# Spreading the DMA transposes of a batch over four head pairs, and placing the sums of the next quad behind different products

## Chip, cores and metric

The kernel runs on one core of one Trainium2 chip. The metric is device time in microseconds (us) of that core; smaller is better. A ratio is the mean time of one kernel's fast runs over the mean of the other's fast runs of the same rounds, so it is not quite the ratio of the medians quoted beside it.

## The reference

Grouped attention, then a feed-forward with a squared ReLU:

```python
# q: 8 x 16 heads x 384 x 64, k and v: 8 x 4 heads x 384 x 64
k = np.repeat(k, 4, axis=1); v = np.repeat(v, 4, axis=1)
scores = np.matmul(q, k.transpose(0, 1, 3, 2)) / 8
scores = scores - scores.max(-1, keepdims=True)
attn = np.exp(scores); attn = attn / (attn.sum(-1, keepdims=True) + 1e-9)
x = np.matmul(attn, v)                    # to 3072 tokens x 1024
h = np.maximum(x @ w_in, 0.0)             # w_in  1024 x 2048
out = (h * h) @ w_out                     # w_out 2048 x 1024
```

## The kernel before

A recorder takes every operation in program order, works out semaphore waits from named keys, and writes one in-order program for each engine. A batch is eight head pairs (`c` = 0 to 7). The feed-forward runs in the same TensorE stream, on two halves of 64 rows side by side: one batch behind attention at first, later two.

Three parts matter here.

First, a batch ahead, q and k are turned by DMA transposes. They are all issued by SyncE, the engine that also issues the transposes `xT` of each pair's attention result and all stores of the output:

```python
def prepare(b):                       # of batch b, one batch ahead
    dup_all_k(b, "gpsimd")            # copies k_st twice into k_dup
    ...dma_start_transpose(kT[b % 2] <- k_dup)                  # all of k
    for part in range(2):
        ...dma_start_transpose(qT[b % 2] half <- q_st[1] half)  # four pairs each

# main loop over head pairs, n = 8 * b + c
    if NPB < n < (B - 1) * NPB:
        if c == (4 if b > 1 else 6):
            prepare(b + 1)
# loads of k, q, v of batch b + 1: once the xT transpose of pair c = 0 has landed
#   row_attend(n - 1, load_next if c == 1 and 2 <= b < B - 1 else None)
```

Second, the down projection of batches 2 to 7 works on quads of blocks with seven products (a Strassen-like scheme) and four sums on VectorE. Where one quad follows another, which happens three times (in the feed-forward of batches 3, 5 and 7), the sums of the following quad are made during the products of the present one:

```python
def rest(q, early, follow):           # products 6, 7, (2), 5, 4 of quad q
    def sums_ahead():
        if follow: sum_part(follow, (1, 2, 3))       # three in a row
    until(sums 1, 2, 3, 4 of q are made)
    ...product 6: y add
    def p7(acc, key):
        add(q["v"], q["u"], acc, key)
        if early: sums_ahead()
    ...
    def c22(acc, key):                # behind product 5
        add(y, q["v"], acc, key); store(y, ...)
        if follow: sum_part(follow, (4,))
    def c21(acc, key): ...            # behind product 4: subtract, store
# then product 1 of the following quad, then product 3 of q (p3: add, store)
```

Third, the output tiles `y_sb` are a fixed ring of six; a store is recorded as soon as its tile is ready:

```python
def next_y():
    ys[0] += 1
    return ys[0] % NY                 # NY = 6
```

The softmax here doesn't subtract the row's maximum and nothing guards it: scores larger than these inputs give would overflow.

## Time and profile before

| | before |
|---|---|
| time, first three runs | 417.27 us median (416.78 to 417.67) |
| span of the profiled run | 415.2 us, granted clock 1.000 |
| TensorE busy | 407.2 us |
| issue time that all matmuls need (worked out below) | 393.2 us |

The page of the kernel before has this for its span, TensorE's share and the chain of work that ended last:

```profile
span 415.2 us, 13254 instructions
...
PE 407.2 (98%) x6061; PEld 307.3 (74%) x6061; DVE 206.6 (50%) x458; ACT 214.1 (52%) x281; POOL 48.7 (12%) x62
...
PE 91%; DVE 4%; ACT 2%; DMA 1%; issue 1%; ACTq 0%; POOL 0%; DVEq 0%
```

TensorE bounds the kernel, but "98% busy" hides slack, because matmuls overlap: the records of one last 376 ns while another starts every 216 ns on the same half. A better measure is the step from one start to the next when nothing holds the stream: 216 ns for 512 columns, 162.5 for 384, 32 for 65. Summed, with two halves side by side, that is 393.2 us. I call it a **stand** when neither half has a matmul in its step, worked out from the start times. I call **head** the time from the span's start to the first scores of batch 1 (35.85 us here), and **rest** what follows (379.37 us).

The first stand that the change aims at. This is the chain of waits of the kernel before near 214 us (start us, us, what):

```profile
210.96 0.69 DVE y_sb L622
211.65 0.61 DVE a_late L622
...
212.90 0.69 DVE h2T L622
...
213.72 0.57 DVE o_sb L527
...
214.33 0.20 PE po L517
```

VectorE adds a product to its output tile, then makes three sums in a row (two into `a_late`, one into `h2T`), and only then gets to `o_sb`, which empties the one PSUM bank `po` that the next attention product needs. TensorE stands 0.69 us. The same happens near 313 us (0.48) and near 398 us (0.46), together 1.63 us.

The second, near 231 us. ScalarE's own timeline in the kernel before (the last bracket is its idle time and what ended it):

```profile
225.40 1.13 ACT L504 ACTIVATE expT<-sc_ps 128x1152 bf16<-128x1152 f32 x1 [1.53 <-PE sc_ps L500]
229.17 0.58 ACT L740 COPY y_sb<-f_ps 128x512 f32<-128x512 f32 x1 [2.64 <-PE po L517]
229.65 1.14 ACT L504 ACTIVATE expT<-sc_ps 128x1152 bf16<-128x1152 f32 x1
```

The releaser in the bracket is misleading: ScalarE's record just before the copy, at 229.11, is a wait for the semaphore of an output store. That store had left SyncE at 221.40 and landed at 229.09, 7.7 us later against a median of 2.3. The copy waits because the ring gives it the tile that was stored last. The Exp behind it is late by as much, and TensorE stands 1.44 us. From 217.6 to 230.3 the load of q for the next batch was under way.

The list of DMA issues has the sizes of the whole run (count, median us from issue to landing):

```profile
qT<-q_next SPq DMA_TRANSPOSE x12, 5.0
...
kT<-k_dup SPq DMA_TRANSPOSE x6, 7.0
```

### The profile page before, as it was taken

To read this page: it belongs to the slowest core of one execution; us is meant where nothing else is said; L and a number is where in the kernel's file an instruction comes from. 1 tells how busy PE (TensorE), PEld (TensorE's weight loads), DVE (VectorE), ACT (ScalarE), POOL (GpSimd) and SP (SyncE) were. 2 spreads that over 40 slices of the span, in tenths; PEclk is the share of its full clock that TensorE was granted. 3 is DMA by queue.
4 is the path that set the end of the run, shared out by engine and by line. 5 is a ranking of instruction groups with operands and counts; after the bars stand their busy time and mean duration, and the time that the engine had idled before them with its cause. 6 is when DMAs were issued, how large, how long until landed. Compare 5 with 4: busy or idle time off the path is not lost.

```text
span 415.2 us, 13254 instructions
## 1 busy us (share of the span) xinstructions
PE 407.2 (98%) x6061; PEld 307.3 (74%) x6061; DVE 206.6 (50%) x458; ACT 214.1 (52%) x281; POOL 48.7 (12%) x62
## 2 busy tenths in 40 slices
PE   8999999999999999999999899999999999999997
PEld 4666888788787787787766688787876788679643
DVE  2664433378332567255563446545654445535453
ACT  4855864377654566546544556555654544214200
POOL 5831002022003000300012000300000000000000
PEclk9999999999999999999999999999999999999999
DMA  8999999859429920991029930496012210020022
GB/s 233 197 197 202 205 190 183 187 80 151 86 87 130 187 70 21 106 226 50 11 82 160 166 108 11 54 199 139 11 48 96 96 47 11 2 101 2 27 77 102
DMA packets 96104, 45.03 MB, mean 108 GB/s; under 512 B 74416, under 2 KB 90032, under 8 KB 96048
## 3 DMA queue, kind: packets, MB, share of 16 engines
q0 software_dynamic: 34288, 16.65, 32.0%
q1 hardware_dynamic: 58720, 25.28, 29.3%
q10 hardware_dynamic: 3040, 2.26, 1.8%
q8 instruction: 47, 0.77, 0.7%
q14 instruction: 9, 0.07, 0.1%
HBM read 35.65 MB, written 12.58 MB: 116 GB/s over the span
## 4 chain that ended last, share of the span: by engine, by line
PE 91%; DVE 4%; ACT 2%; DMA 1%; issue 1%; ACTq 0%; POOL 0%; DVEq 0%
PE sc_ps L558 18%; PE f_ps L558 17%; PE sc_ps L688 12%; PE po L517 12%; PE f_ps L688 11%; PE sc_ps L500 7%; PE sc_ps L604 5%; PE f_ps L604 4%; PE f_ps L843 2%; DMA w_late<-in_q_dram 1%; ACT expT L504 1%; PE po L378 1%; DVE y_sb L622 1%; PE sc_ps L361 1%; PE sc_ps L300 1%
## 5 line engine op out<-in xcount | busy, mean ns | idle before, releaser
L504 ACT ACTIVATE expT<-sc_ps 128x1152 bf16<-128x1152 f32 x112 | 126.5, 1130 | 106.7 <-PE sc_ps L500 64.1
L558 PE MATMUL f_ps<-xT,w_in_sb 64*128 64x384 bf16 x976 | 150.2, 322 | 0.0
L558 PE MATMUL sc_ps<-xT,w_in_sb 64*128 64x384 bf16 x976 | 149.2, 322 | 0.0
L558 PEld LDWEIGHTS sc_ps<-xT,w_in_sb 64*128 64x128 f16 x976 | 81.8, 94 | 16.0
L558 PEld LDWEIGHTS f_ps<-xT,w_in_sb 64*128 64x128 f16 x976 | 82.6, 94 | 13.3
L517 PEld LDWEIGHTS po<-v_aug,expT 64*128 64x128 bf16 x2016 | 77.4, 94 | 12.2 <-DVE o_sb L527 2.2
L568 ACT ACTIVATE h2T<-hr 128x384 bf16<-128x384 f32 x122 | 61.3, 519 | 47.0 <-DVE hr L564 46.5
L517 PE MATMUL po<-v_aug,expT 64*128 64x65 bf16 x2016 | 81.4, 190 | 0.8 <-DVE o_sb L527 0.8
L500 PE MATMUL sc_ps<-qT,kT 64*128 64x384 bf16 x336 | 56.9, 323 | 2.0 <-ACT expT L504 1.8
L564 DVE TENSOR_SCALAR hr<-sc_ps 128x384 f32<-128x384 f32 x61 | 33.9, 556 | 37.1 <-PE sc_ps L558 16.3
L564 DVE TENSOR_SCALAR hr<-f_ps 128x384 f32<-128x384 f32 x61 | 33.9, 556 | 30.1 <-PE f_ps L558 14.5
L688 PE MATMUL sc_ps<-w_late,h2T 64*128 64x512 f16 x176 | 43.5, 376 | 0.0
L604 PE MATMUL sc_ps<-w_out_sb,h2T 64*128 64x512 f16 x192 | 41.6, 376 | 0.0
L604 PE MATMUL f_ps<-w_out_sb,h2T 64*128 64x512 f16 x192 | 40.6, 376 | 0.0
L688 PE MATMUL f_ps<-w_out_sb,a_late 64*128 64x512 f16 x160 | 39.5, 376 | 0.0
L688 PE MATMUL f_ps<-w_out_sb,h2T 64*128 64x512 f16 x144 | 35.4, 376 | 0.0
L688 PE MATMUL sc_ps<-w_out_sb,h2T 64*128 64x512 f16 x144 | 35.4, 376 | 0.0
L525 DVE RECIPROCAL rinv<-po 128x6 f32<-128x6 f32 x56 | 11.0, 196 | 47.0 <-PE sc_ps L604 12.8
L527 DVE TENSOR_TENSOR o_sb<-po,rinv 128x384 bf16<-128x384 f32 x56 | 31.2, 557 | 1.9
L500 PEld LDWEIGHTS sc_ps<-qT,kT 64*128 64x128 bf16 x336 | 25.0, 94 | 8.9 <-ACT expT L504 4.8
L688 PE MATMUL f_ps<-w_late,h2T 64*128 64x512 f16 x112 | 27.2, 376 | 0.0
L688 PE MATMUL sc_ps<-w_out_sb,a_late 64*128 64x512 f16 x112 | 26.9, 376 | 0.3 <-DVE y_sb L622 0.3
(101 smaller groups left out, 418.0 us busy)
## 6 DMA issues: line engine op xcount, KB each, us to landing
out_dram<-y_sb SPq DMA_DIRECT2D x47, 256.0 KB, 2.3
q_next<-in_q_dram POOLq DMA_DIRECT2D x7, 768.0 KB, 10.6
w_in_sb<-in_moe_w_in_dram POOLq DMA_DIRECT2D x8, 512.0 KB, 12.4
w_out_sb<-in_moe_w_out_dram POOLq DMA_DIRECT2D x2, 2048.0 KB, 33.6
k_st<-in_k_dram POOLq DMA_DIRECT2D x7, 192.0 KB, 4.0
v_st<-in_v_dram POOLq DMA_DIRECT2D x7, 192.0 KB, 11.2
xT<-o_sb SPq DMA_TRANSPOSE x56, 2.7
w_late<-in_q_dram ACTq DMA_DIRECT2D x1, 768.0 KB, 8.4
```

Source lines behind the costliest of these rows:

```text
L300: m = pe.matmul(ps[:, t * 128:(t + 1) * 128], src[:, t * 128:(t + 1) * 128], ident[:], is_transpose=True)
L500: "tensor", lambda pe: pe.matmul(sc_ps[:, i, 0:S], kt[rows, j * 128:(j + 1) * 128], qt[rows, :]),
L504: R.add("scalar", lambda e: e.activation(expT[p % NEX][:, 3 * half:3 * half + 3, :], sc_ps[:, 0:3, 0:S], AF.Exp, scale=0.125), reads=[("sc ...
L517: "tensor", lambda pe: pe.matmul(po_v[:, f % NJ, f // NJ, :], expT[p % NEX][rows, 2 * j + f % 2, f // 2 * 128:f // 2 * 128 + 128], v_aug[b ...
L525: R.add("vector", lambda e: e.reciprocal(rinv_v, po_v[:, :, :, D:D + 1]), reads=["po"], writes=[("rinv", p % 2)])
L527: R.add("vector", lambda e: e.tensor_tensor(o_sb[p % NO][:, :, :, :], po_v[:, :, :, 0:D], rinv_v.to_broadcast([128, NJ, 2, D]), ALU.mult), ...
L558: "tensor", lambda pe: pe.matmul(acc[:, 0:S], w_in_sb[rows, kc, c * 128:(c + 1) * 128], xT[b % NXT][rows, kc, :], start=(h == 0 and kc == ...
L564: R.add("vector", lambda e: e.tensor_scalar_max(hr[r][:, :], acc[:, 0:S], 0.0), reads=[key], writes=[("hr", r)])
L568: R.add("scalar", lambda e: e.activation(h2T[b % 2][:, c, :], hr[r][:, :], AF.Square), reads=[("hr", r)], writes=h2(b, c))
L604: "tensor", lambda pe: pe.matmul(acc, h2T[b % 2][rows, c, i * 128:(i + 1) * 128], w_out_sb[rows, c, jj * 512:(jj + 1) * 512], start=(h == ...
L688: "tensor", lambda pe: pe.matmul(acc, lhs[rows], right[rows, c], start=(first and h == 0 and c == 0), stop=(h == 1 and c == NHC - 1), skip ...
L843: m = pe.matmul(acc[:, 0:S], w_in_sb[:, kc, c * 128:(c + 1) * 128], xT[b % NXT][:, kc, :], start=(kc == 0), stop=(kc == NKC - 1))
```

## The change

The intent: shorter bursts on SyncE and on the DMA engines, and no long run of sums on VectorE. The transposes of a batch become six (k in two, q in four), spread over pairs 4 to 7. For batch 2 all six still go out at once, at pair 6, where before three did. The sums 1, 2, 3 and 4 of the following quad go behind products 7, 5, 4 and 3, one each. Product 6 accordingly asks for sums 1 to 3 alone.

```diff
-    def prepare(b):
-        dup_all_k(b, "gpsimd")
-        ...one transpose of k, two of q
+    def turn_k(b, g): ...      # transpose of two k heads
+    def turn_q(b, c): ...      # transpose of two head pairs of q
+    PARTS = [(turn_k, 0), (turn_q, 0), (turn_q, 2), (turn_k, 2), (turn_q, 4), (turn_q, 6)]
+    def prepare(b, parts=range(6)):
+        for i in parts: ...
@@ def p3: behind product 3
             store(q["u"], x0, i0, 1)
+            if follow:
+                sum_part(follow, (4,))
@@ def rest
-                sum_part(follow, (1, 2, 3))
+                sum_part(follow, which)          # ahead(which)
@@ behind product 7 (or 2)
-                sums_ahead()
+                ahead(1)
@@ behind product 5
-            if follow:
-                sum_part(follow, (4,))
+            ahead(2)
@@ behind product 4
+            ahead(3)
@@ main loop
             if c == (4 if b > 1 else 6):
-                prepare(b + 1)
+                dup_all_k(b + 1, "gpsimd")
+            if b == 1 and c == 6:
+                prepare(2)
+            if b > 1 and c >= 4:
+                prepare(b + 1, ((0,), (1, 2), (3, 4), (5,))[c - 4])
```

## The prediction

> **What bounds the kernel now.** TensorE: the page gives PE 98% busy over 415.2 us and 91% of the chain that ended last, at clock 1.00. As busy time of pipelined matmuls hides slack, I counted issue steps from the trace: two 64-row streams run side by side, a matmul every 216 ns (512 columns), 162.5 ns (384) or 32 ns (65). All matmuls together need 393 us. The other 22 us are lost: about 12.5 in the first 40 us, 4 in the last 10, only 5.5 between. The change touches that middle and the start of the tail.
>
> **Gaps it can reach** (both streams idle; start times and the chain of waits):
> 1. Near 214, 313 and 398 us TensorE stands 0.71, 0.52 and 0.54 us, together 1.77. The chain is VectorE: y add 0.69, three sums of the next quad 0.61 + 0.61 + 0.68 in a row, then reciprocal 0.20 and o_sb 0.56 (at 398 the next y add), then the matmul that needs the bank.
> 2. Near 231 us it stands 1.45 us behind an Exp queued behind the ScalarE copy of product 2, which waits for an output store to leave its y buffer: issued 221.4, landed 229.1, 7.7 us against the usual 2.3. From 219 to 226 us the queue of the q load holds the DMA engines.
> 3. About 1.5 us of small gaps (exp latency at 78, 130, 134; others); not addressed.
>
> **What the change does.** Sums: same number and size; one each behind products 7, 5, 4, 3 instead of three behind 7 and one behind 5. VectorE has about 2.7 us between an attend's end and the next one's need of the bank; y add + one sum + reciprocal + o_sb take 2.1, so most of (1) goes: -1.5 us. No product comes close to waiting for its sum.
> Transposes: 3 issues per batch (k about 2.9 us of SyncE, q twice 2.2) become 6, in five of six prepared batches over four head pairs: +18 issues of an estimated 1.2 to 2 us, on SyncE, off the chain. They no longer block SyncE while q lands (a ready store waited 6 us at 230), so xT transposes and stores land earlier, but none of these is on the chain. The late store of (2) was issued before the k transpose and starved by the q load, which stays. The Trainium skill, "DMA: Bandwidth & Descriptors", section "Queues, rings and completion order", says that each DMA engine round-robins between queues per packet and a completion lands only after that engine's earlier writes; the 7.7 us agree with sharing, hardly with fair turns. Indirectly (2) shrinks by about 0.5: with the sums apart, the transpose that triggers the q load comes about 1.2 us earlier, the chain 0.7. PE's 3 more waits per batch hide behind queued matmuls.
>
> **Sum.** -1.5 - 0.5 = -2.0 us: 417.3 to **415.2 us**, 80% range 413.7 to 416.9. Faster by over 2%: 0.01; within 2%: 0.98; slower by over 2%: 0.01.
>
> **What would show it.** The gaps near 213, 312, 397 us gone, VectorE showing y add + one sum; the same matmuls in the same order; a store near 228 us still landing after about 7 us and the ScalarE copy waiting for it, 0.7 to 1.2 us of stall; k transposes 12 (was 6), q 24 (was 12), in all slightly more SyncE issue time; head and end unchanged.
>
> **What would make it wrong.** The store stall vanishing (then about 414) or growing, because the y buffer's need and the q load move against each other; a sum behind product 4 or 3 delaying an o_sb into a new stall of half a us; late k and q parts landing after the next batch's scores need them.

## More of the kernel before

What SyncE does near 70 us, where batch 2 is prepared (its queue in the timeline; x is the number of issues merged in a line):

```profile
64.55 2.59 SPq L331 DMA_TRANSPOSE kT<-k_dup  x1
68.56 3.94 SPq L338 DMA_TRANSPOSE qT<-q_next  x2
72.54 1.56 SPq L396 DMA_TRANSPOSE xT<-o_sb  x1
74.14 2.08 SPq L589 DMA_DIRECT2D out_dram<-y_sb  x3
76.26 2.50 SPq L396 DMA_TRANSPOSE xT<-o_sb  x2
```

The q transposes wait for the q load, which lands at 68.5; then come the `xT` transposes of the last three pairs of batch 1, with three stores between.

## The result, and the profile after

The changed kernel took 416.59 us median (415.77 to 418.48, six runs) against 417.35 (416.71 to 417.67, six runs) of before; ratio 0.9992, 95% interval 0.9969 to 1.0014. That is not the 415.2 predicted. Two later sets of the same kernel, each against the kernel before on the same chip, gave 1.0039 (1.0010 to 1.0068) and 1.0017 (0.9996 to 1.0038). The mean of the three sets is 417.77 us, that of before in the same sets 417.19: if anything, the change costs half a us.

The page of the changed kernel, same three lines:

```profile
span 414.9 us, 13294 instructions
...
PE 406.6 (98%) x6061; PEld 310.9 (75%) x6061; DVE 208.0 (50%) x458; ACT 214.2 (52%) x281; POOL 48.1 (12%) x62
...
PE 91%; DMA 4%; DVE 2%; ACT 2%; ACTq 0%; issue 0%; POOL 0%; DVEq 0%
```

The chain lost half of its VectorE share and got four times the DMA share. The matmuls and their order are the same in the two programs. In this profile the rest of the span fell from 379.37 to 377.71 us, and the head grew from 35.85 to 37.16.

VectorE's timeline of the changed kernel in the place of the first stand:

```profile
213.30 0.69 DVE L630 TENSOR_TENSOR y_sb<-sc_ps,y_sb 128x512 f32<-128x512 f32 x1 [1.55 <-PE po L525]
213.91 0.68 DVE L630 TENSOR_TENSOR a_late<-h2T 128x1024 bf16<-128x1024 bf16 x1
214.51 0.19 DVE L533 RECIPROCAL rinv<-po 128x6 f32<-128x6 f32 x1
214.73 0.56 DVE L535 TENSOR_TENSOR o_sb<-po,rinv 128x384 bf16<-128x384 f32 x1
```

One sum instead of three now stands ahead of `o_sb`. The stands near 214 and 398 us are gone; 0.22 us is left near 313.

The output store near 223 us, in the chain of waits of the changed kernel:

```profile
223.04 6.65 DMA out_dram<-y_sb
...
229.76 0.59 ACT y_sb L748
230.35 1.04 ACT expT L512
...
231.43 0.49 PE sc_ps L508 x3
```

It is still late (6.65 us), and in this profile the stand was 0.39 us. SyncE's queue where batch 2 is prepared:

```profile
65.11 1.22 SPq L331 DMA_TRANSPOSE kT<-k_dup  x1
68.38 3.35 SPq L339 DMA_TRANSPOSE qT<-q_next  x2
71.78 1.29 SPq L331 DMA_TRANSPOSE kT<-k_dup  x1
73.11 3.81 SPq L339 DMA_TRANSPOSE qT<-q_next  x2
76.97 1.26 SPq L404 DMA_TRANSPOSE xT<-o_sb  x1
78.27 1.56 SPq L597 DMA_DIRECT2D out_dram<-y_sb  x3
79.87 2.51 SPq L404 DMA_TRANSPOSE xT<-o_sb  x2
```

From the landing of q (68.4) on, the transposes hold the queue until 76.9 instead of 72.5: q takes four issues instead of two, and the second half of k, which before went out with the first while q was still loading, now waits between them. The last `xT` is issued at 81.1 instead of 77.5. And this is on the chain, in a place where before there was no stand. Chain of waits of the changed kernel:

```profile
80.72 0.40 DVE y_sb L620
81.12 2.37 DMA xT<-o_sb
83.49 0.04 issue
83.53 0.33 PE sc_ps L566
```

Line 566 is the up projection of batch 1; it needs the last `xT` of that batch, and TensorE stands 1.01 us. The list of DMA issues:

```profile
qT<-q_next SPq DMA_TRANSPOSE x24, 3.7
...
kT<-k_dup SPq DMA_TRANSPOSE x12, 4.3
```

Each part lands sooner, as intended; it does not help, because the whole of a batch is not wanted sooner.

### The profile page after: what moved, and what is told of

The parts are those of the page before. It is cut to its first block, busy times and chain, and to the rows that moved or that the text cites. A ratio compares the mean times of both kernels' runs of the same rounds, so it can differ in the third digit from the quotient of the medians.

```text
span 414.9 us, 13294 instructions
## 1 busy us (share of the span) xinstructions
PE 406.6 (98%) x6061; PEld 310.9 (75%) x6061; DVE 208.0 (50%) x458; ACT 214.2 (52%) x281; POOL 48.1 (12%) x62
## 4 chain that ended last, share of the span: by engine, by line
PE 91%; DMA 4%; DVE 2%; ACT 2%; ACTq 0%; issue 0%; POOL 0%; DVEq 0%
PE sc_ps L566 18%; PE f_ps L566 17%; PE f_ps L696 12%; PE sc_ps L696 12%; PE po L525 12%; PE sc_ps L508 7%; PE sc_ps L612 5%; PE f_ps L612 4%; DMA w_late<-in_q_dram 2%; DMA out_dram<-y_sb 2%; PE f_ps L854 2%; PE po L386 1%; ACT expT L512 1%; PE sc_ps L369 1%; PE sc_ps L300 1%; DMA xT<-o_sb 1%
## 5 line engine op out<-in xcount | busy, mean ns | idle before, releaser
L525 PEld LDWEIGHTS po<-v_aug,expT 64*128 64x128 bf16 x2016 | 77.4, 94 | 10.8 <-DVE o_sb L535 0.9
L533 DVE RECIPROCAL rinv<-po 128x6 f32<-128x6 f32 x56 | 10.9, 195 | 46.1 <-PE sc_ps L612 12.8
## 6 DMA issues: line engine op xcount, KB each, us to landing
q_next<-in_q_dram POOLq DMA_DIRECT2D x7, 768.0 KB, 10.8
w_in_sb<-in_moe_w_in_dram POOLq DMA_DIRECT2D x8, 512.0 KB, 11.9
```

What stands on the lines that cost most here:

```text
L525: "tensor", lambda pe: pe.matmul(po_v[:, f % NJ, f // NJ, :], expT[p % NEX][rows, 2 * j + f % 2, f // 2 * 128:f // 2 * 128 + 128], v_aug[b ...
L533: R.add("vector", lambda e: e.reciprocal(rinv_v, po_v[:, :, :, D:D + 1]), reads=["po"], writes=[("rinv", p % 2)])
```

## The experiments

My theory after the result (A): the moved sums are worth 1.4 to 1.5 us; the six transposes of batch 2 at once cost about 1 us; the late store and the head vary by chance. Rivals: all of the new loss is chance (B), or the sums or the smaller transposes themselves cost time (C).

The table has one profile of each run, in us. For e1 to e4 these are the first profiles, with spans of 417.0, 414.2, 415.5 and 414.7 us; the traces that are kept for these four are of other executions (416.0, 413.3, 415.8 and 415.2 us). The kept ones are a second sample, given below the table. "Sums" adds the stands near 214, 313 and 398; "84", "97" and "231" are the other stands that differ; "mean" is over all runs of that set, "before" that of the kernel before in the same set.

| kernel | head | rest | sums | 84 | 97 | 231 | mean | before |
|---|---|---|---|---|---|---|---|---|
| before | 35.85 | 379.37 | 1.63 | 0 | 0 | 1.44 | 417.24 | |
| e5 before again | 35.94 | 378.93 | 1.63 | 0 | 0 | 1.00 | 417.12 | 416.97 |
| e9 before, one instruction more | 36.30 | 379.99 | 1.63 | 0 | 0.66 | 1.31 | 417.00 | 417.48 |
| e14 before, v load later | 36.49 | 378.74 | 1.64 | 0 | 0 | 0.80 | 417.69 | 417.39 |
| e6 before, tiles in order of stores | 36.34 | 377.82 | 1.63 | 0 | 0 | 0 | 416.01 | 416.97 |
| e3 six parts only | 35.91 | 379.63 | 1.63 | 0.91 | 0 | 0.82 | 418.14 | 416.95 |
| e2 sums only | 36.27 | 377.90 | 0.22 | 0 | 0 | 1.57 | 417.17 | 416.95 |
| the change | 37.16 | 377.71 | 0.22 | 1.01 | 0 | 0.39 | 416.89 | 417.23 |
| e1 the change again | 38.16 | 378.81 | 0.22 | 0 | 0 | 2.52 | 418.57 | 416.95 |
| e13 the change, third set | 36.66 | 378.36 | 0.23 | 0.54 | 0 | 1.48 | 417.86 | 417.39 |
| e4 change, batch 2 mended | 36.67 | 377.99 | 0.22 | 0 | 0 | 1.70 | 416.66 | 416.95 |
| e11 e4, loads a pair earlier | 36.13 | 376.20 | 0.23 | 0 | 0 | 0 | 415.28 | 417.48 |
| e10 change, tiles in order | 36.58 | 377.14 | 0.23 | 0.73 | 0 | 0 | 415.76 | 417.48 |
| e8 e4, tiles in order | 36.48 | 376.18 | 0.23 | 0 | 0 | 0 | 414.81 | 416.97 |
| e7 sums only, tiles in order | 38.02 | 376.24 | 0.23 | 0 | 0 | 0 | 414.75 | 416.97 |
| e12 e7 again | 36.07 | 376.99 | 0.23 | 0 | 0.66 | 0 | 414.59 | 417.48 |
| e15 e7, more warm-up | 36.77 | 377.00 | 0.22 | 0 | 0.66 | 0 | 415.46 | 417.39 |

The table checks itself: take the 376.2 us of e8 as a base, add 1.4 where the sums are not moved, and add the stands 84, 97 and 231; every rest comes out within 0.45 us. The kept traces of e1 to e4, read in the same way, do so too:

| kept trace | head | rest | sums | 84 | 97 | 231 |
|---|---|---|---|---|---|---|
| e1 the change again | 36.64 | 379.36 | 0.22 | 1.87 | 0 | 1.11 |
| e2 sums only | 35.97 | 377.30 | 0.22 | 0 | 0 | 0.94 |
| e3 six parts only | 36.58 | 379.22 | 1.63 | 0.78 | 0 | 0.52 |
| e4 change, batch 2 mended | 36.79 | 378.39 | 0.23 | 0 | 0.66 | 1.34 |

### e1, the changed kernel again

No edit.

> The changed kernel once more, to separate chance from cause. In the first profile of it the head (span start to the first scores of batch 1) took 37.2 us against 35.9 before, and the rest 377.7 against 379.4. Theory A (the head is chance of the first DMAs, the 1.0 us stand of TensorE near 84 us is caused by the change): the head comes out anywhere from 35.5 to 37.5 us, the rest again at 377.7 within 0.3, the stand near 84 us is there again with 0.7 to 1.3 us, those near 214 and 398 us are gone. Rival B (the stand near 84 us is chance too): it is absent or of another size, and the rest is near 376.7. Rival C (the change itself slows the head): the head is 37 us again. Time 416.0 to 417.3 us.

Measured: ratio 1.0039, rest 378.81, head 38.16, none near 84 us, 2.52 near 231 us. Both the stand near 84 and the rest missed theory A's numbers. The stand near 84 is not fixed: the q load that opens SyncE's burst landed at 68.8 us, as in the first profile (68.4), since it sits behind the weight loads on the DMA queue and not behind TensorE (in the kept traces it landed at 68.0 to 69.8 us whatever the head; at 68.6 in e7 with a head of 38.02). With a head 1.0 us later TensorE comes 1.0 us later to an `xT` that lands even earlier (82.9 against 83.5). Counted from the end of the head, the last `xT` landed 46.33 us on in the first profile (stand 1.01), 46.22 in e3 (0.91), 46.04 in e10 (0.73), 45.86 in e13 (0.54) and 44.73 in e1 (none): in each case the stand is the landing less 45.3 us, where TensorE needs it. In the kept traces of kernels without the six at once it landed at 42.5 to 44.3, always in time. So a late head hides this stand, and a late q load makes it longer: in the kept trace of e1 q landed at 69.7 us, the last `xT` 47.25 us after the head, and TensorE stood 1.87 us in two pieces (0.85 and 1.02, for the last two `xT`). In that of e3 it was 46.09 and 0.78.

### e2, sums only

The transposes as before; the rest of the diff stays.

> Only the move of the sums; transposes as before (three at once). Theory A: the sums are worth about 1.5 us and, through the earlier q load, part of the store stall; no stand near 84 us. Rest of the span 376.7 to 377.2 us (before 379.4), stands near 214 and 398 gone, 231 between 0.3 and 1.2. Time about 2 us under before when the head is equal. Rival C (what the first result gave back came from the sums, not the transposes): a stand near 84 us also here, rest 377.7. A smaller stand near 231 than 0.9 would mean that the sums, not the spread transposes, took that stall away.

Measured: rest 377.90, no stand near 84, sums' stands 0.22 instead of 1.63, near 231 us 1.57. Time 416.68 median, ratio 1.0006 (0.9984 to 1.0027). The sums do what was predicted, to a tenth; the store stand did not shrink in this profile (0.94 in the kept trace; the kernel before had 1.44 and 1.00). The rival that the sums make the stand near 84 falls. The time of this set is not faster than before. Two of its six runs (419.23 and 418.09 us) had a lowered clock; what else took the gain back in the runs without a trace is not shown, the head and the store being the likely places (see e7, and the clock below).

### e3, six parts only

The sums as before; the transposes as in the change.

> Only the six parts of the transposes; sums as before. Theory A: the stand near 84 us is there (0.7 to 1.3 us), those near 214, 313 and 398 us as before (together about 1.65), 231 near the 1.44 of before, since the late store was issued ahead of any transpose; rest 380.2 to 380.6 us, so about 1 us slower than before with an equal head. Rival (the spread transposes took the store stall away): 231 shrinks to about 0.4, and the rest is near 379.4.

Measured: stand near 84 us 0.91, near 231 us 0.82, rest 379.63; time 417.97 median, ratio 1.0033 (1.0020 to 1.0046). The parts alone make the kernel slower, by 1.2 us in the mean (418.14 - 416.95), and bring the stand near 84 with them. The rest came out better than expected because the store stand was smaller, as it can be in the kernel before too (e14: 0.80; 0.52 in the kept trace of e3, with a rest of 379.22).

### e4, batch 2's last parts behind the last xT

```diff
             if b == 1 and c == 6:
-                prepare(2)
+                prepare(2, (0, 1, 2))
+            if b == 2 and c == 0:
+                prepare(2, (3, 4, 5))
```

> The changed kernel with the last three of batch 2's six parts issued behind the last two xT transposes of batch 1 (same transposes, same bytes, another place in SyncE's order). Theory A (SyncE works in order, so the last xT, which the feed-forward of batch 1 waits for, is issued 3.6 us later than before): the last xT is issued near 77.5 us instead of 81.1, the stand near 84 us is gone, rest 376.6 to 376.9 us, about 1 us less than the changed kernel. Rival (six smaller transposes load the DMA engines more, whatever their order): the stand stays at 0.5 us or more.

Measured: the stand near 84 us is gone. SyncE's queue in this kernel:

```profile
71.50 1.26 SPq L404 DMA_TRANSPOSE xT<-o_sb  x1
72.80 3.19 SPq L597 DMA_DIRECT2D out_dram<-y_sb  x3
76.03 2.52 SPq L404 DMA_TRANSPOSE xT<-o_sb  x2
78.59 1.29 SPq L331 DMA_TRANSPOSE kT<-k_dup  x1
```

The same six transposes of the same bytes, in another place in the order, and the last `xT` is issued at 77.3. So it was the order on SyncE and not the load on the DMA engines. The kept trace agrees: last `xT` issued at 77.8, no stand near 84. The rest was 377.99 and not 376.6 to 376.9, all of it because the store stand was 1.70 here.

### e5, control: the kernel before again

No edit.

> Control: the kernel before, unchanged, in the place of a variant. So far the variants' runs scatter over 1.7 to 4.9 us each, those of before over 1.1. Theory A (the scatter comes from the landing of the first inputs and of the late store, which are chance, in every kernel): ratio 1.000 within 0.003, the head (35.9 us in the one profile of before) anywhere from 35.5 to 38, the stand near 231 us anywhere from 0.4 to 2.5 us. Rival (the change itself makes head and stand unsteady): head 35.9 and stand 1.4 again within 0.2, all runs within 416.5 to 417.7 us.

Measured: ratio 1.0006 (0.9992 to 1.0019), all runs 416.67 to 417.58, head 35.94, store stand 1.00. Neither theory is met whole: the store stand moves by 0.4 between two profiles of one kernel, but head and times of the kernel before are steady. The scatter of the changed kernels is larger and asks for a reason.

### e6, the kernel before with tiles in the order of their stores

```diff
-    ys = [0]
+    ys = list(range(NY))
     def next_y():
-        ys[0] += 1
-        return ys[0] % NY
+        return ys.pop(0)
@@ def store
+        if c1 == 512:
+            ys.append(y)
```

Every tile is stored once, so the tile handed out is the one whose store was issued longest ago.

> The kernel before, with the y buffers handed out in the order in which their stores were issued instead of in a fixed ring, so that the ScalarE copy of product 2 takes a buffer whose store is long done. Theory A (that copy waits for the store behind the q load, and nothing else holds the Exp near 231 us): the stand near 231 us is gone, the others (214: 0.69, 313: 0.48, 398: 0.46) stay; rest 377.9 to 378.1 us, 1.4 us under before. Rival (the Exp would be late anyway, behind DMAs): the stand stays over 0.7 us.

Measured: no stand near 231 us, the others unchanged, rest 377.82; ratio 0.9980 (0.9966 to 0.9994). The copy now starts at 227.40, its store dependence gone, while the store after product 3 still landed 7.0 us after its issue. So the wait for the tile was all that held the Exp.

### e7 and e12, moved sums and tiles in order, transposes as before

The edits of e2 and e6 together.

> The moved sums, transposes as before, y buffers in the order of their stores. Theory A (sums -1.5 us, store stall -1.4 us, independent): rest 376.2 to 376.5 us against 379.4 of before, and less scatter than the sums alone. If the gain of the sums is given back in the late store, as the sums-only runs suggest (416.7 against 416.9), this one shows the full 3 us: ratio 0.992 to 0.994 with an equal head. Rival (the sums' gain is given back elsewhere): rest over 377 us.

Measured: rest 376.24 (3.1 us under before), ratio 0.9949 (0.9933 to 0.9965), 414.36 us median, all runs 414.21 to 416.05. The profiled run was the slowest, with a head of 38.02 us. With the tiles in order, the sums show their worth in the time too: 414.75 against 416.01 for e6 in the same set, 1.3 us.

> The fastest kernel again: a second sample of its time and of the head. Rest 376.2 within 0.2; ratio 0.993 to 0.996; time 414.2 to 416.1 us, those over 415.5 with a late head or a clock of 0.996.

Measured: ratio 0.9930 (0.9915 to 0.9946), 414.52 us median, 414.04 to 415.49. The rest was 376.99 and not 376.2, because of a stand of 0.66 us near 97 us, which e9 has too, in the kernel before (its cause is in the last section). This is the fastest kernel, and faster than both kernels compared.

### e8, the change mended, with tiles in order

The edits of e4 and e6.

> The whole change, batch 2's last three parts behind the last xT transposes of batch 1, y buffers in the order of their stores. Theory A (with batch 2 mended the six parts cost and give nothing, as no transpose is on the chain): rest 376.2 to 376.5 us, the same as with the sums and the buffers alone, within 0.2. Rival (the spread parts have a worth of their own): 0.5 us or more below that.

Measured: rest 376.18, ratio 0.9951 (0.9936 to 0.9965), 414.76 us median. Against e7 (rest 376.24; 414.75 us in the mean, here 414.81) the spread transposes give nothing and, once batch 2 is mended, cost nothing.

### e9, the kernel before with one instruction more

```diff
+            R.add("vector", lambda e: e.memset(warm[:, 0:1], 0.0), writes=["warm"])
```

> The kernel before with one VectorE instruction more (it clears one column of a tile that nothing reads any more, near 125 us), so that VectorE's program is one entry longer, as it is in every kernel with the moved sums. Question: in 7 of 36 runs with the moved sums the mean clock was 0.995 or 0.996 and in none of about 50 runs without them; in the two such profiles the first v load landed about 1 us late, TensorE stood 1.1 us at 8 us, and the clock was half for 3.4 us in the head. Theory A (chance of the first loads): this kernel as before, 416.3 to 417.9 us, head about 36, clock 1.000 in all runs; and that would leave the link with the moved sums unexplained. Rival (any change of the program's layout can do it): one or more runs of clock 0.996, mean ratio over 1.002.

Measured: 416.57 to 418.08 us, clock 1.000 in all five runs, head 36.30. Ratio 0.9982 (0.9966 to 0.9998) for a kernel that does the same work: a warning that such intervals are a little too narrow here. A longer VectorE program alone does not make the head slow.

### e10, the whole change with tiles in order

The edit of e6 on the changed kernel.

> The whole change with the y buffers in the order of their stores, batch 2's six parts at once as the change has them. Set against the mended one (414.8 us mean, rest 376.2) it shows the price of the six at once without the scatter of the late store. Theory A: stand near 84 us of 1.0 us less what the head is later than 36.9 us or so, rest 376.2 plus that stand; time 415.3 to 415.8 us mean. Rival (no price): 414.8.

Measured: stand near 84 us 0.73, rest 377.14 (with one more stand of 0.20 near 238 us), mean 415.76. In the same rounds e12, without the six parts, had 414.59: the six at once cost 1.2 us in the mean, about the stand that the profiles show.

### e11, the loads a pair earlier

On e4, with the ring as before:

```diff
-load_next if c == 1 and 2 <= b < B - 1 else None
+load_next if c == (1 if b == 2 else 0) and 2 <= b < B - 1 else None
```

> The mended change (batch 2's last parts behind the last xT) with the loads of the next batch triggered one head pair earlier for batches 4 to 7; y buffers in the ring as before. If the late store near 221 us is held up by the q load and by nothing else, it now lands within 3 us or by 226 us, ahead of the need near 228, and the stand near 231 us falls under 0.2 us: rest 376.2 to 376.6 us, the same as with the other order of buffers. Rival (the store is late because of xT and k transposes on the same queue): it still lands after 6 us or more.

Measured: the q load now runs from 211.4 to 222.4 us; the late store, issued at 221.0, landed at 226.6; the copy still waited for it, but started at 226.72 and no stand followed. ScalarE's timeline:

```profile
226.72 0.59 ACT L748 COPY y_sb<-f_ps 128x512 f32<-128x512 f32 x1 [0.68 <-DMA out_dram<-y_sb]
227.21 1.14 ACT L512 ACTIVATE expT<-sc_ps 128x1152 bf16<-128x1152 f32 x1
```

Rest 376.20, ratio 0.9947. The landing took 5.7 us and came at 226.6, neither within 3 us nor by 226 as I had named, but early enough for the Exp. Moving the load alone takes the stand away, and the order of SyncE's issues is the same as in e4, so the load is what makes the store late enough to matter.

The packets in the traces say more about how. In the sixteen kept traces other than e11's the first packet of the store moved only 4.0 to 5.9 us after its issue, within 2 us of the landing of the `xT` transpose that SyncE had issued 3.2 to 3.6 us ahead of it. That transpose itself took 6.6 to 9.5 us, against a median of 2.7. So the store stands behind a transpose on SyncE's own queue that the load slows as well. Whether it would be in time without that transpose ahead of it was not tried.

### e13, e14, e15: the head

> The changed kernel a third time; its two ratios so far were 0.9992 and 1.0039. Theory A (sums -1.5, six at once +0.7 to +1.0, late store 0 to +1, head +0.5 on average): ratio 0.999 to 1.003, mean 416.8 to 418.5 us, stand near 84 us of 0 to 1.1 (less with a late head), stand near 231 anywhere from 0.4 to 2.5. A ratio under 0.997 would mean that the second result was the odd one.

Measured: ratio 1.0017 (0.9996 to 1.0038), mean 417.86, stands 0.54 and 1.48, head 36.66. All within what was expected; the first result was the lucky one of three.

e14 swaps two loads at the start of the kernel before: the first v load goes behind that of the last three k heads.

```diff
-    R.add("scalar", ...load of v_f...)
     first_k(1, 4, "scalar")
+    R.add("scalar", ...load of v_f...)
```

> The kernel before with the first v load issued behind the load of the last three k heads instead of ahead of it, so that v lands near 7.7 to 8.2 us instead of 7.0. Theory A (a late v makes TensorE stand near 8 us for about 1 us, a half clock of 3.4 us follows, the head grows by 1 to 2 us, with no change of the sums at all): head 37 to 38.2 us, clock 0.996 in some or all runs, mean 418 us or more. Rival (the head is longer only with the moved sums, for another reason): head 36.0 to 36.5, clock 1.000, mean 417.2.

Measured: v landed at 8.08 us (6.87 before) and TensorE stood 0.92 us, but the head of the profiled run was 36.49 with a clock of 0.999. The theory that a late v is enough for a head of 38 us falls in this profile. The six runs went from 415.94 to 419.54 us, though, where the kernel before in the same set went from 416.69 to 418.43, and one of them, the slowest, had a mean clock of 0.995.

e15 adds six warm-up matmuls to e7 ahead of the first attend:

```diff
-            idle(2 if n == 1 else 1)
+            idle(8 if n == 1 else 1)
```

> The kernel with moved sums and ordered buffers, with six more warm-up matmuls (0.1 us each) ahead of the first attend, where TensorE stood for 1.1 us in the slow heads. Theory A: no run with a clock of 0.996, heads all within 36.0 to 37.0 us, runs within 414.0 to 415.5. Cost where v is early: at most 0.3 us, as that head waits for the loads anyway. Rival (the clock drops for another reason, or the late loads cost the time without it): one or more runs over 415.9 us or with 0.996.

Measured: head 36.77, no run with a lowered clock, but 414.60 to 416.62 us and 415.46 in the mean, against 414.75 and 414.59 for e7 and e12. The drop did not happen in six runs, which six runs cannot prove, and no gain from the warm-up is shown.

What a slow head looks like. Two stretches of e7's profiled run, whose mean clock was 0.996 (stretch, length, then busy us of TensorE, its weight loads, VectorE, ScalarE and GpSimd, each with its count, then the granted clock, the DMA share and GB/s):

```profile
6.00:12.00 6.00, 4.24 (x43) 2.19 (x43) 1.61 (x5) 3.35 (x6) 3.89 (x6) 0.90 1.19 279
12.00:18.00 6.00, 5.96 (x71) 3.58 (x69) 2.61 (x9) 4.99 (x7) 4.71 (x8) 0.82 1.53 195
```

The clock record has a stretch of half clock from 10.8 to 14.2 us. Ahead of it TensorE had waited 1.07 us for v and 0.56 us for q. Lowered clocks of this kind (0.995 or 0.996) came in 9 of 60 runs of kernels with moved sums (e15 left out) and in none of 65 runs of kernels without them, e14 left out. Six of the nine came on the one chip that ran e1 to e4 (six of 18 runs there with moved sums, none of 17 without). I found no way in which sums made over 100 us later could do this: the head's operations and waits are the same in both programs. In the profiles of the first table kernels with the sums moved also had the longer heads without a lowered clock (36.1 to 37.2 against 35.9 to 36.3). The kept traces of e1 to e4 don't bear that out: 35.97, 36.64 and 36.79 with moved sums, 36.58 without. So a longer head is not shown to come with the moved sums; the lowered clocks came more often with them, on that chip above all, though e14 had one without. Why this is so stays open.

## Why the prediction was wrong

- **The sums: right.** Predicted -1.5 us; the stands went from 1.63 to 0.22 us in every profile, and the rest from 377.82 (e6) to 376.24 (e7).
- **"None of these is on the chain": this step failed.** It counted 18 more issues "on SyncE, off the chain", and noted that for one batch all still go out at once, but did not follow that batch. There SyncE's order puts the last `xT` of batch 1, which the up projection waits for, behind all six transposes. Measured: stands of 1.01, 0, 0.54, 0.91 and 0.73 us in the five profiles with six at once (1.87 and 0.78 in the kept traces of e1 and e3), none in the others; 1.2 us in the mean time (e3 against before, e10 against e12). e4 shows that it is the order.
- **"Indirectly (2) shrinks by about 0.5": this gain did not come, and the term may have had the wrong sign.** The trigger of the q load did come earlier, by what I said. But the store did not land earlier with it. From the q load's issue to the store's landing it took 10.6 to 11.5 us (mean 11.0) in the six kept traces without moved sums and 10.9 to 13.2 us (mean 11.9) in the ten with them (e11, whose loads are moved, left out). In the ring kernels the stand was 0.80 to 1.44 us (mean 1.07) in five profiles without, 0.39 to 2.52 us (mean 1.53) in five with moved sums; with the kept traces of e1 to e4 added, the means are 0.98 of six and 1.38 of eight. The ranges overlap so far that a larger stand is not shown, only that the 0.5 was not gained. A likely reason, argued and not shown by itself: the store ahead of it, of product 4, used to leave SyncE before the q load began and land in 2.0 us; with the load earlier both run together, and it takes 3.9 to 4.5. That the load is the cause of the late store as such is shown by e11, and that the ring turns it into a stand by e6. The warning in the prediction ("the y buffer's need and the q load move against each other") was the right one; the number was not.
- **"Head and end unchanged": the head was not.** In three profiles of the change it took 36.7 to 38.2 us (mean 37.33; 37.16 with the kept trace of e1, 36.64), in two of the kernel before 35.85 and 35.94. That is 1.3 to 1.4 us, about as much as the sums gave, from code that is the same. The size is that of these few profiles; the cause is open, and it need not come with the sums: e7 kept 1.3 us of their 1.6 against e6 in the mean time.

The sum for the changed kernel, from three profiles of it against two of before: rest 378.29 - 379.15 = -0.86 us, head 37.33 - 35.90 = +1.43, together +0.57; the mean times say 417.77 - 417.19 = +0.58. That the two agree to 0.01 is luck: with the kept trace of e1 the sum is -0.59 + 1.26 = +0.67. The gain of the sums was given back in a queue's order and in the head; that of the store never came.

## What to carry to other kernels

When a transfer is cut into parts, look at the one place where the parts still go out together, and at what stands behind them in the same in-order queue: it is the time of the issues ahead of the waiting one that counts there, not the bytes moved. Before counting a gain in one stand, ask what ends the next one: where that is a DMA landing, earlier arrival may only make TensorE wait longer for it. Take more than one profile before explaining a stand: here the same kernel showed 0, 0.54, 1.01 and 1.87 us in one place. And give out buffers in the order in which they come free, not in a fixed ring: here that cost nothing, was worth 1.0 us by itself, and let the other gain be seen.

## What the Trainium skill lacked or had wrong

- **"DMA: Bandwidth & Descriptors", section "Queues, rings and completion order".** It says that each DMA engine takes turns between queues, packet by packet. Sharing is what the runs show, equal shares are not: a 256 KB store beside a 768 KB load of q (384 bytes to a packet of the trace) took 6.6 to 8.8 us instead of 2.0 (e11, whose load ends earlier, left out). In the kept traces its first packet moved 4.0 to 5.9 us after the issue, and it landed between 0.5 us behind the load's end and 2.2 us ahead of it. The page has no such figure for a small store beside a large load.
- **"TensorE: Matmul & The Clock Gate", section "What's actually happening".** It gives half clock "after ≥1 idle window (~3.4µs)". In e7 the drop followed waits of only 1.07 and 0.56 us with matmuls between them, and lasted 3.4 us. In e14 a wait of 0.92 us brought no drop. By start times TensorE stood 1.96 of the 3.41 us ahead of the drop in e7, and 1.60 us in the same place of the changed kernel's first profile, without a drop. So partly idle windows can do it, and the page doesn't say how idle.
- **"SBUF — State Buffer", section "Who interferes with whom".** It says that a VectorE instruction with two SBUF inputs and a GpSimd instruction that reads SBUF lock each other out, and that the order of issue decides who waits. This is the stand near 97 us, and it agrees. In e12 the GpSimd copy starts at 92.90 and the VectorE operation at 93.18 takes 1.95 us; in e7, where the VectorE operation started 0.20 us ahead of the copy, the same operation took 0.69. VectorE's and GpSimd's timelines in e12:

```profile
92.58 0.68 DVE L623 TENSOR_TENSOR w_late<-w_late,w_out_sb 128x1024 f16<-128x1024 f16 x1
93.18 1.95 DVE L623 TENSOR_TENSOR w_late<-w_out_sb 128x1024 f16<-128x1024 f16 x1
```

```profile
92.90 1.69 POOL L325 COPY k_dup<-k_st 128x1536 bf16<-128x1536 bf16 x1 [2.01 <-DMA k_st<-in_k_dram]
```

  What the page lacks is how little decides it: a shift of a few tenths of a us, which came by chance in 4 of the 17 kept traces (copy 0.2 to 0.4 us ahead, operation 1.95 us) and cost TensorE 0.66 us each time.
- No page has the time that the issue of an SBUF-to-SBUF DMA transpose of these sizes holds SyncE. In the kept traces it was 1.18 us in the median for three blocks of 128 x 128 (all seventeen), 1.29 for six (eight traces with six parts) and 2.54 for twelve (nine with three transposes a batch), and up to 5.0 us beside loads. So two halves take as long as the whole, but never under 1.2 us each.
